# Converting float64 weights on the chip: the sign enters with the integer addition instead of in a pass of its own

## The chip, the cores and the metric

The kernel runs on one core of a Trainium2 chip. What counts is the device time of one execution in microseconds (us). The engines of the core are named as in the profile: PE (TensorE, matmuls; PEld is its weight load), DVE (VectorE), ACT (ScalarE), POOL (GpSimd) and SP (SyncE, which only issues DMAs here).

## The reference, cut to what matters

A causal attention with decay over 4 batches of 8 heads (576 rows, 64 columns each), followed by two feed-forward layers without bias:

```python
attn = softmax(q @ k.T / 8 + decay, causal) @ v      # -> x of 2304 x 512
x = square(relu(x @ w_in)) @ w_out                   # 512 -> 2048 -> 512
h = x @ w2_in
out = where(h >= 1, h, where(h <= -1, 0, (h + 1)**2 / 4)) @ w2_out
```

The four weight matrices reach the kernel as float64, seen as pairs of 32-bit words. The kernel turns each number into a float32 and then into a sum of two numbers that PE takes (a high and a low part), so that three matmuls stand for one precise product.

## The kernel before, in words

The 2304 rows are cut into five blocks of 512, 512, 512, 512 and 256 columns of PE's moving operand. Each block goes through 32 steps: 16 for the first layer pair and 16 for the second. A step is 12 matmuls into `h` (line 1009), an activation on ACT and DVE (lines 1027 to 1040, and the difference `gl` on line 586 or 588), and, two steps later, 12 matmuls into the four accumulators (lines 1060 to 1062). The attention of a block runs between the steps of the block ahead of it. For the first 256 rows of a head it is `attention32` (matmuls on lines 646, 675 and 689), for the others `attention`.

Only block 0 meets weights that are still float64. For each of its steps one piece of up to 1024 columns is loaded (`raw`), decoded (`decode`, into `wf`), and split into its high and low part (`w_split`, into `whl`). `whl` is used from SBUF in that step, and also stored in DRAM (`scr`), from where blocks 1 to 4 load it again. So all decoding lies in the first 262 us. There are 34 pieces: most of 1024 columns, a few of 512.

A piece is decoded in these passes over its columns, where `lo` and `hi` are the two words of a float64:

- `o1` (line 940 on ACT or 941 on DVE): the absolute value of `hi`, into `wf`.
- `o2` (line 944 on ACT or 945 on POOL): the top bits of `lo`, scaled down, into `low`.
- `o3` (line 948, DVE): clamp between F32_MIN and F32_MAX.
- `o4` (line 950, DVE): shift left by 5, then right by 2.
- `o5` (line 952, DVE): sign and top exponent bit, masked out of `hi`, are put in with an "or".
- the addition (line 955 on DVE or 956 on POOL): `wf` plus `low`, as integers.

Then `w_split` copies the high part (line 574 on ACT, 577 on DVE) and subtracts it (line 586 on DVE, 588 on POOL). There is one `low` buffer, two `wf` buffers, and six buffers that `raw` and `whl` share.

No order is written out by hand. Each operation names the engines that it could run on, with an assumed cost for each; `Schedule.improve` plays the whole program through with several sets of weights, chooses engine and order for every operation, and the program is emitted in that order. Any change of an operation or of a cost can therefore move operations all over the kernel.

Of the kernel before, what the change touches and what calls it, by code (L numbers as in the profile page):

```python
# [8 lines left out]
F32 = mybir.dt.float32  # L9
F32R = mybir.dt.float32r  # L10
F16 = mybir.dt.float16
BF16 = mybir.dt.bfloat16
I32 = mybir.dt.int32
U32 = mybir.dt.uint32
U64 = mybir.dt.uint64
AF = mybir.ActivationFunctionType
ALU = mybir.AluOpType
# [4 lines left out]
P = 128  # L22
# [37 lines left out]
def pattern(bits):  # L60
    return struct.unpack("f", struct.pack("I", bits))[0]


F32_MIN = pattern(0x38100000)
F32_MAX = pattern(0x47EFFFFF)


# [278 lines left out]
def act_t(n, psum=False, ptr=0):  # L346
    return n / 1200.0 + (0.05 if psum else 0.095) + 0.095 * ptr


def dve_t(n):  # L350
    return n / 960.0 + 0.07


def dve2_t(n):
    return n / 1920.0 + 0.065


def pool_t(n):
    return n / 1200.0 + 0.18


def pool2_t(n):
    return n / 467.0 + 0.13
# [17 lines left out]
def tile_attention_moe_moe(ctx: ExitStack, tc: tile.TileContext, qkv, f, blank, w2, outT):  # L381
    nc = tc.nc
    PSUM = bass.MemoryType.PSUM
    W64 = w2.dtype == U64
    sch = Schedule()
    const = ctx.enter_context(tc.tile_pool(name="const", bufs=1))
# [8 lines left out]
    def new(tag, name, shape=None, dt=None, kind=None):  # L395
        p, tp, sh, d = pools[tag]
        shape = sh if shape is None else shape
        kw = {"padded_shape": sh} if list(shape) != list(sh) and len(shape) == len(sh) and dt is None else {}
        return Buf(p, lambda: tp.tile(shape, dt or d, tag=tag, name=name, **kw), kind)
# [50 lines left out]
    for blk in range(5):  # L450
        lo, hi = (T_LO, T_START) if blk == 0 else (V[NFC * ATTENTION[blk][0]], V[NFC * ATTENTION[blk][1]] - 6)
# [12 lines left out]
    mask = const.tile([P, OFF + P], BF16, name="mask")  # L464
    half = const.tile([P, 1], F32, name="half")
    warm = const.tile([P, 1], F32, name="warm")
    ident = const.tile([P, P], F32, name="ident")
    Q2 = [const.tile([P, REST], F32R, name=f"Q2_{i}") for i in range(2)]
    K2 = [const.tile([P, S], F32R, name=f"K2_{i}") for i in range(2)]

    QK = [new("PT", f"QK{i}", [P, QUAD * 2 * HEAD], F32) for i in range(2)]

    def setup():
        sb = new("x", "setup", [P, 2 * NKC * 512], F32)
# [2 lines left out]
        lb = lambda a=D, z=P, c=0, m=1: sb.tile[a:z, 4 * S + HEAD * c:4 * S + HEAD * (c + m)]  # L477
        due = -100.0
        G, V_, A = nc.gpsimd, nc.vector, nc.scalar
        oh = sch.op(due - 10, {"POOL": (0.05, lambda: G.memset(warm, 0.5))})  # L480
        oh = sch.op(due - 10, {"ACT": (1.5, lambda: A.activation(warm, warm, AF.Ln))}, [oh])

        bs = []
        for i, (a, z) in enumerate(((0, 1), (1, QUAD))):
            n = (z - a) * HEAD
# [8 lines left out]
        o2 = sch.op(due - 5, {"POOL": (0.55, lambda: G.memset(onesf(0, P), 1.0))}, bufs=[sb])  # L494
        sch.op(due + 90, {"POOL": (0.05, lambda: G.memset(half, 0.5))})
        o3 = sch.op(due, {"DVE": (0.37, lambda: V_.tensor_scalar(
            fr(), fr(), 1e-4, 1.0, op0=ALU.max, op1=ALU.min))}, [o1], [sb])
        o4 = sch.op(due, {"ACT": (0.58, lambda: A.activation(lf(), fr(), AF.Ln))}, [o3, oh], [sb])
        o5 = sch.op(-98.5, {"DVE": (0.67, lambda: V_.tensor_tensor_scan(
            cum(), onesf(), lf(), 0.0, op0=ALU.mult, op1=ALU.add))}, [o4, o2], [sb])  # L500
        sch.op(due, {"ACT": (1.4, lambda: A.activation(warm, warm, AF.Exp))}, [o4, *bs])
        hi = lambda: fr().bitcast(F32R)
        lo = lambda: lf().bitcast(F32R)
        o6 = sch.op(due + 125, {"DVE": (0.37, lambda: V_.tensor_copy(hi(), cum()))}, [o5], [sb])
# [6 lines left out]
        def first_rows(head, row, out, deps):  # L511
            return sch.op((-101, -99, 8, 8)[head], {"DVE": (0.61, lambda: V_.tensor_tensor_scan(
                out(), onesf(row, row + 1, HEAD), lb(row, row + 1, head), 0.0, op0=ALU.mult, op1=ALU.add))},
                [bs[head > 0], o2, *deps], [sb, QK[0]])

        zs = {}
        due = 100.0
# [33 lines left out]
    def clear(i, half):  # L551

        n = QUAD * HEAD
        rows = lambda a, z: QK[i].tile[a:z, n * half:n * half + n]
        kq = lambda a, z, t: rows(a, z).rearrange("p (c t n) -> p c t n", t=2, n=HEAD)[:, :, t, :]
        if i + half:
            return [sch.op(-90, {"SP": (dma_t(D * n * 4), lambda: nc.sync.dma_start(out=rows(D, P), in_=blank))},
                           [], [QK[i]], early=BE[2 * i + half - 1])]
        fill = lambda out, x: {"DVE": (n / 1920 + 0.01, lambda: nc.vector.memset(out(), x))}
# [10 lines left out]
    def copies(out, in_, n, engines="ACT DVE POOL", psum=False):  # L570

        alts = {}
        if "ACT" in engines:
            alts["ACT"] = (act_t(n, psum), lambda: nc.scalar.activation(out(), in_(), AF.Copy))  # L574
        if "DVE" in engines:
            alts["DVE"] = (
                dve_t(n) if psum else dve2_t(n), lambda: nc.vector.tensor_copy(out(), in_()), *([] if psum else [True]))
        if "POOL" in engines:
            alts["POOL"] = (pool_t(n), lambda: nc.gpsimd.tensor_scalar(  # L579
                out(), in_(), 1.0, 0.0, op0=ALU.mult, op1=ALU.add))  # L580
        return alts

    def subs(out, a, b, n, engines="DVE POOL"):
        alts = {}
        if "DVE" in engines:
            alts["DVE"] = (dve_t(n), lambda: nc.vector.tensor_sub(out(), a(), b()), True)  # L586
        if "POOL" in engines:
            alts["POOL"] = (pool2_t(n), lambda: nc.gpsimd.tensor_sub(out(), a(), b()))  # L588
        return alts
# [302 lines left out]
    scr_op, raw, wf, whl, whl_op, new_pairs = {}, {}, {}, {}, {}, {}  # L892

    def span(layers):
        return slice(layers[0], layers[-1] + 1)

    def w_load(s):
# [10 lines left out]
        if first:  # L908
            b = new("big", f"raw{s}", [P, 2, 512], U64) if W64 else new("wf", f"wf{s}")
            loads = []  # L910
# [20 lines left out]
    def decode(words, y, n, due, loads, rb, w):  # L931


        lo, hi = lambda: words()[:, :, 0], lambda: words()[:, :, 1]
        yi = lambda: y().bitcast(I32)
        lb = new("low", f"low{w.order}")
        part = lambda: lb.tile[:, :n]
        v = nc.vector
        o1 = sch.op(due, {
            "ACT": (act_t(n), lambda: nc.scalar.activation(y(), hi().bitcast(F32), AF.Abs)),  # L940
            "DVE": (dve2_t(n), lambda: v.tensor_scalar(yi(), hi(), 0x7FFFFFFF, None, op0=ALU.bitwise_and), True),
        }, loads, [rb, w])
        o2 = sch.op(due, {
            "ACT": (act_t(n), lambda: nc.scalar.activation(part(), lo().bitcast(U32), AF.Copy, scale=2.0 ** -29)),
            "POOL": (pool_t(n), lambda: nc.gpsimd.tensor_scalar(
                part(), lo().bitcast(U32), 2.0 ** -29, 0.0, op0=ALU.mult, op1=ALU.add)),
        }, loads, [rb, lb])
        o3 = sch.op(due + 0.6, {"DVE": (dve2_t(n), lambda: v.tensor_scalar(
            y(), y(), F32_MIN, F32_MAX, op0=ALU.max, op1=ALU.min), True)}, [o1], [w])
        o4 = sch.op(due + 1.2, {"DVE": (dve2_t(n), lambda: v.tensor_scalar(  # L950
            yi(), yi(), 5, 2, op0=ALU.logical_shift_left, op1=ALU.logical_shift_right), True)}, [o3], [w])
        o5 = sch.op(due + 2.4, {"DVE": (dve_t(n), lambda: v.scalar_tensor_tensor(  # L952
            yi(), hi(), -0x40000000, yi(), op0=ALU.bitwise_and, op1=ALU.bitwise_or), True)}, [o4], [rb, w])
        return sch.op(due + 4.8, {
            "DVE": (dve_t(n) + 0.07, lambda: v.tensor_tensor(yi(), yi(), part(), op=ALU.add), True),  # L955
            "POOL": (pool2_t(n), lambda: nc.gpsimd.tensor_tensor(yi(), yi(), part(), op=ALU.add)),
        }, [o5, o2], [lb, w])

    def w_decode(s):
        if s not in raw:  # L960
# [13 lines left out]
    def w_split(s):  # L974

        if s not in wf:
            return
        c = span(sorted(layer for layers in new_pairs[s].values() for layer in layers))
        n = 512 * (c.stop - c.start)
        w = wf.pop(s)  # L980
        if s not in whl:
            whl[s] = new("big", f"whl{s}")
        b = whl[s]
        due = V0(s + 2) - 4.5
        hi, lo = (lambda i=i: b.tile[:, c, i, :] for i in range(2))
        o = sch.op(due, copies(hi, lambda: w.tile[:, c], n, "ACT DVE"), whl_op[s], [w, b])
        o = sch.op(due + 1, subs(lo, lambda: w.tile[:, c], lambda: hi().bitcast(F32), n), [o], [w, b])
        whl_op[s].append(o)
        for pair, layers in new_pairs[s].items():
            c_ = span(layers)  # L990
            store = sch.op(due + 6, {"SP": (dma_t(P * 4096 * len(layers)), lambda c_=c_, pair=pair: nc.sync.dma_start(
                out=scr[pair][:, c_], in_=b.tile[:, c_].bitcast(F32)))}, [o], [b])
            for layer in layers:
                scr_op[pair, layer] = store
# [200 lines left out]
```

## Time and profile before

| | us |
|---|---|
| median of 3 runs | 969.46 (968.41 to 970.44) |
| the profiled execution, its time | 967.33 |
| the profiled execution, its span | 965.6 |
| PE busy | 939.4 (97%) |
| ACT busy | 631.0 (65%) |
| DVE busy | 605.0 (63%) |
| POOL busy | 192.6 (20%) |

The span is the part of the time that the trace covers. Busy shares are averages over stages: DVE is busy nine tenths or more of nearly every slice up to 260 us, and between one and seven tenths after that. A matmul's record is longer than the distance to the next one, since matmuls overlap, so that small gaps of PE don't show as idle time. Records of neighbours on DVE and ACT overlap a little too.

### The profile page before, as it was taken

What the parts mean: (1) busy time and instruction counts of PE and PEld (TensorE: products, weight loads), DVE (VectorE), ACT (ScalarE), POOL (GpSimd) and SP (SyncE); (2) the same over time, 40 slices, a digit from 0 to 9 for tenths busy, and PEclk for the clock granted to TensorE, in tenths of its full rate; (3) what the DMA queues carried; (4) which work ended last, traced back from release to release, by engine and by line L of the source; (5) the groups of instructions that cost most, each with busy time, mean ns of one, the idle gap of its engine ahead of it and who ended that gap; (6) DMA issues with size and microseconds to landing.
All of it is one profiled execution on the core that took longest, in us unless ns stands there. A gap on an engine that the chain in (4) does not pass through costs nothing.

```text
span 965.6 us, 14315 instructions
## 1 busy us (share of the span) xinstructions
PE 939.4 (97%) x4758; PEld 782.6 (81%) x4758; DVE 605.0 (63%) x1338; ACT 631.0 (65%) x1274; POOL 192.6 (20%) x329
## 2 busy tenths in 40 slices
PE   6999999998999999999999999999999999999998
PEld 4767777766778888888888888888888888889998
DVE  7999999999966868767677767776311132220032
ACT  5999888777676777877677777776433343334354
POOL 4210202232223233333222222332000000002200
PEclk7999999999999999999999999999999999999999
DMA  7789998987999898898799888888565555559993
GB/s 190 244 283 411 365 346 299 318 327 270 360 263 325 249 275 229 249 277 255 210 291 265 270 274 208 234 255 220 196 224 209 178 203 190 188 205 354 370 377 142
DMA packets 126618, 255.77 MB, mean 265 GB/s; under 512 B 89880, under 2 KB 90800, under 8 KB 104592
## 3 DMA queue, kind: packets, MB, share of 16 engines
q1 hardware_dynamic: 126544, 254.85, 82.3%
q8 instruction: 38, 0.62, 0.3%
q14 instruction: 36, 0.29, 0.1%
HBM read 195.40 MB, written 38.45 MB: 242 GB/s over the span
## 4 chain that ended last, share of the span: by engine, by line
PE 80%; DVE 9%; DMA 3%; issue 2%; ACT 2%; SPq 0%; POOL 0%; DVEq 0%; ACTq 0%; POOLq 0%
PE h L1009 35%; PE acc L1060 12%; PE acc L1062 12%; PE acc L1061 12%; PE av L846 4%; PE s L767 2%; PE s L768 2%; DVE wf L952 2%; DMA PT<-PP 2%; DVE whl L586 1%; DVE wf L955 1%; DVE gl L586 1%; DVE wf L950 1%; DMA out_dram<-o 1%; ACT whl L574 1%
## 5 line engine op out<-in xcount | busy, mean ns | idle before, releaser
L1009 PE MATMUL h<-x,whl 128*128 128x512 f32 (+1 forms) x1896 | 433.6, 372 | 7.9 <-DVE whl L586 6.4
L1009 PEld LDWEIGHTS h<-x,whl 128*128 128x128 f32 x1896 | 324.7, 189 | 66.2 <-DVE whl L586 9.4
L1060 PE MATMUL acc<-gh,whl 128*128 128x512 f32 (+1 forms) x640 | 239.8, 375 | 2.3 <-ACT o L574 2.3
L1062 PE MATMUL acc<-gl,whl 128*128 128x512 f32 (+1 forms) x640 | 236.9, 370 | 0.3 <-DVE gl L586 0.2
L1061 PE MATMUL acc<-gh,whl 128*128 128x512 f32 (+1 forms) x640 | 236.4, 369 | 0.2 <-DVE whl L586 0.2
L586 DVE TENSOR_TENSOR gl<-g,gh 128x512 fp32r<-128x512 f32 (+1 forms) x119 | 79.6, 669 | 113.3 <-PE acc L1062 81.7
L1062 PEld LDWEIGHTS acc<-gl,whl 128*128 128x128 f32 x640 | 120.7, 189 | 21.9 <-DVE gl L586 0.7
L1060 PEld LDWEIGHTS acc<-gh,whl 128*128 128x128 f32 x640 | 120.8, 189 | 21.5 <-ACT o L574 3.2
L1061 PEld LDWEIGHTS acc<-gh,whl 128*128 128x128 f32 x640 | 120.8, 189 | 16.1 <-DVE whl L586 0.7
L588 POOL TENSOR_TENSOR gl<-g,gh 128x512 fp32r<-128x512 f32 (+1 forms) x41 | 45.9, 1120 | 287.7 <-PE acc L1062 214.5
L1040 DVE SCALAR_TENSOR_TENSOR g<-r,h 128x512 f32<-128x512 f32 (+1 forms) x80 | 50.5, 631 | 80.3 <-ACT r L1038 79.5
L1027 ACT ACTIVATE r<-h 128x512 f32<-128x512 f32 (+1 forms) x80 | 44.0, 550 | 84.1 <-PE h L1009 81.4
L1036 ACT ACTIVATE r<-h,half 128x512 f32<-128x512 f32 (+1 forms) x80 | 51.2, 640 | 65.4 <-PE h L1009 64.2
L821 DVE SCALAR_TENSOR_TENSOR PP<-E,st,PP 128x512 f16<-128x512 f32 (+2 forms) x128 | 75.1, 620 | 12.0 <-ACT PP L817 11.6
L784 ACT ACTIVATE E<-E,st 64x320 f32<-64x320 f32 (+2 forms) x96 | 63.7, 664 | 25.5 <-DVE st L593 16.9
L817 ACT ACTIVATE PP<-E,st 128x512 f16<-128x512 f32 (+2 forms) x128 | 68.9, 591 | 9.0 <-DVE st L791 4.6
L593 DVE CUSTOM_DVE_ANT_0 E<-s,mask 128x288 f32<-128x288 f32 (+2 forms) x128 | 61.9, 500 | 20.0 <-PE s L768 17.4
L846 PEld LDWEIGHTS av<-pr,vt 128*128 128x128 f32 x288 | 53.2, 188 | 13.6 <-ACT r L1036 1.4
L574 ACT ACTIVATE gh<-g 128x512 fp32r<-128x512 f32 (+1 forms) x73 | 42.5, 582 | 32.0 <-DVE g L1040 31.8
L846 PE MATMUL av<-pr,vt 128*128 128x320 f32 (+2 forms) x288 | 61.8, 287 | 0.9 <-DVE st L593 0.7
L574 ACT ACTIVATE pr<-PT 128x640 fp32r<-128x640 f16 (+2 forms) x64 | 37.0, 587 | 30.3 <-DMA PT<-PP 25.7
L579 POOL TENSOR_SCALAR pr<-PT 128x640 fp32r<-128x640 f16 (+2 forms) x45 | 29.4, 657 | 117.6 <-PE av L846 56.4
(251 smaller groups left out, 1148.5 us busy)
## 6 DMA issues: line engine op xcount, KB each, us to landing
whl<-scr SPq DMA_DIRECT2D x112, 1024.0 KB
raw<-in_w_dram SPq DMA_DIRECT2D x28, 1024.0 KB
scr<-whl SPq DMA_DIRECT2D x28, 1024.0 KB
in<-in_qkv_dram SPq DMA_DIRECT2D x32, 608.0 KB
whl<-scr SPq DMA_DIRECT2D x32, 512.0 KB
out_dram<-o SPq DMA_DIRECT2D x16, 256.0 KB
QK<-in_qkv_dram SPq DMA_DIRECT2D x7, 512.0 KB
raw<-in_w_dram SPq DMA_DIRECT2D x6, 512.0 KB
```

Of the source, the lines that this page charges most:

```text
L574: alts["ACT"] = (act_t(n, psum), lambda: nc.scalar.activation(out(), in_(), AF.Copy))
L586: alts["DVE"] = (dve_t(n), lambda: nc.vector.tensor_sub(out(), a(), b()), True)
L593: return nc.vector.tensor_tensor_reduce(out=out, in0=ps, in1=mask[:m, OFF - q0:OFF - q0 + n], scale=scale, scalar=3e38, op0=ALU.add, op1=A ...
L784: nc.scalar.activation(Ec.tile[:m, :e], Ec.tile[:m, :e], AF.Exp, scale=-1.0, bias=nmx(), accum_out=st.tile[:m, 1, ci:ci + 1])))}, [*tops, ...
L817: nc.scalar.activation(hi, x, AF.Copy, scale=r())
L821: nc.vector.scalar_tensor_tensor(lo, x, r(), hi, op0=ALU.mult, op1=ALU.subtract)
L846: nc.tensor.matmul(av.tile[:, c0:W], vt.tile[:, kc, :, :], pr.tile[:, i, :n], start=(kc == 0 and i == 0), stop=(kc == NK - 1))
L1009: nc.tensor.matmul(ps.tile[:, :n], w.tile[:, 0, wi, kc * P:(kc + 1) * P], src.tile[:, kc, xi, :n], start=(kc == 0 and i == 0), stop=(kc == ...
L1036: o1 = sch.op(due, {"ACT": (act_t(n, True, 1), lambda: A.activation(r.tile[:, :n], ps(), AF.Relu, scale=0.5, bias=half))}, [o], [psb, r])
L1060: nc.tensor.matmul(a.tile[:, :n], wh, gh.tile[:, :n], start=(fc == 0), stop=False)
L1061: nc.tensor.matmul(a.tile[:, :n], wl, gh.tile[:, :n], start=False, stop=False)
L1062: nc.tensor.matmul(a.tile[:, :n], wh, gl.tile[:, :n], start=False, stop=(fc == NFC - 1))
```

## The change

`o5` is gone. A new pass `o6` fills the upper 16 bits of each word of `low` with the sign and the constant exponent bits 0x3F80, either on ACT (the function Sign, written as bf16, which is 0x3F80 or 0xBF80; a small `tiny` is added so that zero counts as positive) or on DVE (mask and "or" on the topmost 16-bit quarter of the float64). `o2` writes only the lower 16 bits of `low`, and its second engine is DVE in place of POOL. `o4` shifts left by 3 and no longer right. So the one integer addition puts in sign, exponent and low bits. Because the decoded number is now half of what it was, `w_split` doubles it: its copy gets a scale, and its subtraction becomes a `scalar_tensor_tensor` on DVE, with POOL no longer a choice. `tiny` is filled once by POOL at the start.

```diff
-F32_MIN = pattern(0x38100000)
+F32_MIN = pattern(0x38200000)
...
+        tiny_op.append(sch.op(due - 9, {"POOL": (0.05, lambda: G.memset(tiny, 2.0 ** -30))}))
...
         o2 = sch.op(due, {
-            "ACT": (act_t(n), lambda: nc.scalar.activation(part(), lo().bitcast(U32), AF.Copy, scale=2.0 ** -29)),
-            "POOL": (pool_t(n), lambda: nc.gpsimd.tensor_scalar(
-                part(), lo().bitcast(U32), 2.0 ** -29, 0.0, op0=ALU.mult, op1=ALU.add)),
+            "ACT": (act_t(n), lambda: A.activation(part16(0), lo().bitcast(U32), AF.Copy, scale=2.0 ** -29)),
+            "DVE": (dve2_t(n), lambda: v.tensor_scalar(
+                part16(0), lo().bitcast(U32), 2.0 ** -29, None, op0=ALU.mult), True),
         }, loads, [rb, lb])
+        o6 = sch.op(due, {
+            "ACT": (act_t(n, ptr=1), lambda: A.activation(
+                part16(1).bitcast(BF16), hi().bitcast(F32), AF.Sign, bias=tiny)),
+            "DVE": (dve2_t(n), lambda: v.tensor_scalar(
+                part16(1), words16()[:, :, 3], 0x8000, 0x3F80, op0=ALU.bitwise_and, op1=ALU.bitwise_or), True),
+        }, [*loads, *tiny_op], [rb, lb])
...
         o4 = sch.op(due + 1.2, {"DVE": (dve2_t(n), lambda: v.tensor_scalar(
-            yi(), yi(), 5, 2, op0=ALU.logical_shift_left, op1=ALU.logical_shift_right), True)}, [o3], [w])
-        o5 = sch.op(due + 2.4, {"DVE": (dve_t(n), lambda: v.scalar_tensor_tensor(
-            yi(), hi(), -0x40000000, yi(), op0=ALU.bitwise_and, op1=ALU.bitwise_or), True)}, [o4], [rb, w])
+            yi(), yi(), 3, None, op0=ALU.logical_shift_left), True)}, [o3], [w])
...
-        }, [o5, o2], [lb, w])
+        }, [o4, o2, o6], [lb, w])
...
-        o = sch.op(due, copies(hi, lambda: w.tile[:, c], n, "ACT DVE"), whl_op[s], [w, b])
-        o = sch.op(due + 1, subs(lo, lambda: w.tile[:, c], lambda: hi().bitcast(F32), n), [o], [w, b])
+        src, unit = lambda: w.tile[:, c], 2.0 if W64 else 1.0
+        o = sch.op(due, {
+            "ACT": (act_t(n), lambda: nc.scalar.activation(hi(), src(), AF.Copy, scale=unit)),
+            "DVE": (dve2_t(n), lambda: nc.vector.tensor_scalar(hi(), src(), unit, None, op0=ALU.mult), True),
+        }, whl_op[s], [w, b])
+        o = sch.op(due + 1, {"DVE": (dve_t(n), lambda: nc.vector.scalar_tensor_tensor(
+            lo(), src(), unit, hi().bitcast(F32), op0=ALU.mult, op1=ALU.subtract), True)}, [o], [w, b])
```

## Rows read from the trace of the kernel before

**Rows 1.** The page's first part: engine, busy us (share of the span), instructions.

```profile
PE 939.4 (97%) x4758; PEld 782.6 (81%) x4758; DVE 605.0 (63%) x1338; ACT 631.0 (65%) x1274; POOL 192.6 (20%) x329
```

**Rows 2.** Busy time by stretch; the first line names the columns.

```profile
core 0: us, PE busy (x) PEld busy (x) DVE busy (x) ACT busy (x) POOL busy (x), PEclk, DMA share, GB/s
26.00:260.00 234.00, 224.34 (x1073) 172.75 (x1074) 226.12 (x416) 196.40 (x375) 48.31 (x48) 1.00 0.88 320
...
80.00:100.00 20.00, 20.00 (x95) 15.67 (x95) 18.98 (x28) 18.27 (x28) 1.29 (x1) 1.00 0.98 391
```

**Rows 3.** The chain that ended last: start us, us, what it spent them on.

```profile
45.55 1.15 DVE wf L952
...
49.98 1.14 DVE whl L586
```

**Rows 4.** Waits, 20 to 260 us: us in total, times, longest us.

```profile
POOL low L945 <- DVE wf L955: 81.3, 9, 17.8
...
PE h L1009 <- DVE whl L586: 6.4, 7, 1.6
```

**Rows 5.** The chain again, where no weights are decoded: two neighbouring steps.

```profile
711.62 2.72 PE h L1009 x12
...
717.07 2.72 PE h L1009 x12
```

**Rows 6.** PE's timeline: first matmul of step 0 and of step 32.

```profile
38.25 0.94 PE L1009 MATMUL h<-x,whl-2_523 128*128 128x512 f32 x3
...
253.69 1.07 PE L1009 MATMUL h<-x,whl 128*128 128x512 f32 x4
```

**Rows 7.** PE and PEld busy in these stretches, lines 1009, 646, 675, 689 in turn.

```profile
38.00:253.60 215.60, 100.27 (x384) 69.49 (x385) 1.00 0.89 325
...
44.00:253.60 209.60, 11.27 (x54) 8.96 (x54) 1.00 0.88 323
...
44.00:253.60 209.60, 8.89 (x51) 6.59 (x51) 1.00 0.88 323
...
44.00:253.60 209.60, 9.16 (x72) 3.83 (x72) 1.00 0.88 323
```

**Rows 8.** Busy by stretch of lines 952 (DVE), 945 (POOL), 944, 940 (ACT).

```profile
26.00:260.00 234.00, 40.35 (x33) 1.00 0.88 320
...
26.00:260.00 234.00, 15.94 (x13) 1.00 0.88 320
...
26.00:260.00 234.00, 21.15 (x19) 1.00 0.88 320
...
26.00:260.00 234.00, 35.75 (x32) 1.00 0.88 320
```

**Rows 9.** Timeline of DVE and ACT: start us, duration us, instruction.

```profile
93.06 1.06 ACT L574 ACTIVATE whl<-wf 128x1024 fp32r<-128x1024 f32 x1 [1.12 <-issue]
93.61 0.70 DVE L950 TENSOR_SCALAR wf<-wf 128x1024 int32<-128x1024 int32 x1
94.03 1.14 ACT L944 ACTIVATE low<-raw 128x1024 int32<-128x1024 uint32 x1
94.22 1.22 DVE L586 TENSOR_TENSOR whl<-wf,whl 128x1024 fp32r<-128x1024 f32 x1
...
95.36 1.22 DVE L952 SCALAR_TENSOR_TENSOR wf<-raw,wf 128x1024 int32<-128x1024 int32 x1
```

**Rows 10.** Groups by line: count, busy us, mean ns, idle before.

```profile
L941 DVE TENSOR_SCALAR wf-1_322<-raw-1_258 128x512 int32<-128x512 int32 x1 | 0.4, 418 | 0.0
L588 POOL TENSOR_TENSOR whl-2_523<-wf-2_249,whl-2_523 128x512 fp32r<-128x512 f32 x1 | 1.3, 1312 | 0.6 <-DVE whl-2_523 L577 0.6
L1036 ACT ACTIVATE r<-h,half 128x512 f32<-128x512 f32 x16 | 10.9, 682 | 5.3 <-PE h L1009 5.2
L1027 ACT ACTIVATE r<-h 128x512 f32<-128x512 f32 x17 | 10.0, 588 | 0.9 <-PE h L1009 0.7
L501 ACT ACT_TABLE_LOAD x1 | 1.3, 1283 | 0.0
```

More of the change, by code (lines that the diff above doesn't have):

```diff
@@ L14 @@
 U32 = mybir.dt.uint32
+U16 = mybir.dt.uint16
 U64 = mybir.dt.uint64
@@ L466, in tile_attention_moe_moe @@
     warm = const.tile([P, 1], F32, name="warm")
+    tiny = const.tile([P, 1], F32, name="tiny")
     ident = const.tile([P, P], F32, name="ident")
@@ L471, in tile_attention_moe_moe @@
     QK = [new("PT", f"QK{i}", [P, QUAD * 2 * HEAD], F32) for i in range(2)]
+    tiny_op = []
     def setup():
@@ L937, in decode @@
         part = lambda: lb.tile[:, :n]
-        v = nc.vector
+        part16 = lambda i: part().bitcast(U16).rearrange("p (n t) -> p n t", t=2)[:, :, i]
+        top = lambda: hi().bitcast(U32)
+        v, A = nc.vector, nc.scalar
         o1 = sch.op(due, {
-            "ACT": (act_t(n), lambda: nc.scalar.activation(y(), hi().bitcast(F32), AF.Abs)),
+            "ACT": (act_t(n), lambda: A.activation(y(), hi().bitcast(F32), AF.Abs)),
             "DVE": (dve2_t(n), lambda: v.tensor_scalar(yi(), hi(), 0x7FFFFFFF, None, op0=ALU.bitwise_and), True),
@@ L943, in decode @@
         o2 = sch.op(due, {
-            "ACT": (act_t(n), lambda: nc.scalar.activation(part(), lo().bitcast(U32), AF.Copy, scale=2.0 ** -29)),
-            "POOL": (pool_t(n), lambda: nc.gpsimd.tensor_scalar(
-                part(), lo().bitcast(U32), 2.0 ** -29, 0.0, op0=ALU.mult, op1=ALU.add)),
+            "ACT": (act_t(n), lambda: A.activation(part16(0), lo().bitcast(U32), AF.Copy, scale=2.0 ** -29)),
+            "DVE": (dve2_t(n), lambda: v.tensor_scalar(
+                part16(0), lo().bitcast(U32), 2.0 ** -29, None, op0=ALU.mult), True),
         }, loads, [rb, lb])
+        o6 = sch.op(due, {
[4 more added lines that the diff above has]
+        }, [*loads, *tiny_op], [rb, lb])
+        words16 = lambda: words().rearrange("p n t -> p (n t)").bitcast(U16).rearrange("p (n t) -> p n t", t=4)
         o3 = sch.op(due + 0.6, {"DVE": (dve2_t(n), lambda: v.tensor_scalar(
```

## The prediction, made before the changed kernel had run

> **What bounds the kernel now.** I read the page's busy line first, then the stage in which weights are decoded, then the chain and the waits of that stage, then PE's pace with and without decoding. The busy line says that PE is the limit: 97% of the span, DVE 63% [rows 1]. That average hides two stages. From 26 to 260 us DVE is busy 226.12 of 234 us (97%) and ACT 196.40 (84%), while PE has 9.7 us without a record [rows 2]. After that DVE is mostly free, and the edit touches nothing there. So the change is worth what it brings before 260 us. The chain agrees: near the start it runs from one decoding pass on DVE to the next, line 952 among them [rows 3]; the only wait of PE for decoded weights that the list of waits shows is small, 6.4 us [rows 4].
>
> How much can PE gain there? Undisturbed, a step starts 5.45 us after the one ahead of it (717.07 - 711.62) [rows 5]. Steps 0 to 31 are 384 matmuls into `h`, all recorded, and take from 38.25 to 253.69, that is 215.4 us [rows 6, 7]. 32 x 5.45 are 174.4; the attention matmuls among them add 11.27 + 8.89 + 9.16 = 29.3 [rows 7]. That is 203.7, so PE loses 11.7 us. Since attention's records overlap a little, and the last passes reach past step 32, I put the most that can come back at 15.
>
> **The change part by part, from 26 to 260 us.** A pass costs the distance to the next start, a little less than its record: DVE's quick pass (line 950) of 1024 columns is 0.70 us long and the next starts 0.61 later, its plain one 1.22 and 1.14; on ACT the next starts 0.97 after a pass of 1.06 [rows 9]. So I take 0.09 off each record.
>
> `o5` goes: 33 passes, 40.35 us of records less 33 x 0.09, which is 37.4 off DVE [rows 8]. `o4` keeps its form, and so does the addition; I cost the fewer bits that they handle at nothing. The subtraction in `w_split` turns from tensor_tensor (1.22) into scalar_tensor_tensor (1.22, as line 952) [rows 9]: nothing. POOL did it for one half-wide piece (1.31) [rows 10]; on DVE that is about half of 1.14, so 0.6. DVE without the new passes: 226.1 - 37.4 + 0.6 = 189.3.
>
> New to ACT and DVE are 46 passes: 33 of `o6`, and the 13 of `o2` that POOL did [rows 8]. On ACT, `o2` costs 21.15/19 - 0.09 = 1.02 and `o6` 35.75/32 - 0.09 = 1.03 and the price of the bias read from `tiny`. The rows show no Sign; a pass of 512 columns with such a bias takes 682 ns and one without 588 [rows 10], so I add 0.09. The mean over 46 is 1.09. On DVE no row shows 16-bit halves read or written with gaps between them. The nearest is line 941, which reads every second 32-bit word: 418 ns for 512 columns [rows 10], the pace of 0.70 for 1024. Its distances in bytes are those of `o6`, so I take 0.61; the other end is the plain pace, 1.13. Neither end allows a gain: the passes weren't there.
>
> If a of the 46 go to DVE, DVE has 189.3 + 0.61 a and ACT 196.4 + 1.09 (46 - a). Both are 210 at a = 34. Against today's 226.1 that takes 16 us off the busiest engine. At 1.13 they meet at a = 26 and 218.5, and 7.6 come off. It turns at 27 passes on ACT, 19 on DVE: there ACT has 226, what DVE has now. All 46 on ACT would be 246.5.
>
> [...]
>
> What takes a wait: `low` is a single buffer, and `o2` waits for the last addition to let go of it. Today that wait is mostly POOL's, 81.3 us in all, and costs nothing, since little stands behind it [rows 4]. On ACT, what queues behind a waiting `o2` or `o6` is Relu and Square of `h`, for which PE's second half-step waits; on DVE, `gl`, with the same waiter. The planner places it late enough in its own times; a wait on the chip costs at most the rest of one addition, 1.2 us. `raw` is free again earlier, after `o1`, `o2` and `o6` rather than behind three DVE passes, so SP can issue the next load earlier. DMA carries that: 320 GB/s over the stage, 391 in its fullest stretch [rows 2], and 15 us less make 320 x 234/219 = 342. The memset of `tiny` stands ahead of little on POOL, about 0.1 us, in a time when PE waits for attention's loads.
>
> Before 26 us two half-wide pieces are decoded: their `o5` goes and two short `o6` come. I cost that at nothing, bounded by 0.7 us a piece either way.
>
> **The sum.** DVE loses 16 us of load, PE can take back 11.7 to 15. Two engines at 210 of a stage of some 225 us are both over 90% busy, and each piece passes from one to the other five times, so some waits stay. I take two thirds of 11.7: 8 us. The profiled execution would go from 967.33 to 959.3; the median of the runs lies 2.1 above the profiled one, so 969.46 becomes 961.5.
>
> **The rivals.**
>
> ACT becomes the bound (slower). In the rows the planner put 32 of `o1`'s passes on ACT in this stage, where DVE was a choice too [rows 8]; for it speaks that habit, against it that DVE's place is then emptier and its pass cheaper. From 27 of 46 passes on ACT there is no gain; at 36 ACT has 235.6, 9.5 us over today's bound, and PE waits for `r` and `gh`: 979. All 46 give 20 us: 990.
>
> Nothing comes of it. PE has few gaps in view, 6.4 us of wait for `whl` [rows 4], and the planner lays the whole kernel out anew: what DVE gives up could be lost where attention's passes now fall. Price: 2 us either way, 967.5 to 971.5.
>
> All comes back: PE runs at its own pace through the stage, 12 to 16 us, so 953.5 to 957.5.
>
> The half-word passes run at the plain pace or slower: 7.6 off the bound in place of 16, half of the forecast's gain, 965.5.
>
> Sign needs another table than Exp. Abs, Relu, Square, Copy and Exp follow the load on line 501 with no other, and a load takes 1.28 us [rows 10]. If Sign isn't in that table, each Sign between other functions costs two loads, 2.57 us. With 15 of them on ACT, 38 us come to an engine near its limit: some 30 us more, 1000.
>
> [...]
>
> **How the numbers follow.** Forecast, 4 to 12 us gained: 0.50. All comes back: 0.13. Plain pace: 0.10. Nothing: 0.15. ACT the bound: 0.09. Tables: 0.03. A measurement of this kernel can tell about 0.2% (1.9 us) from no change. Faster: 0.50 + 0.13 + 0.09 + a fifth of 0.15, 0.75. Same: two thirds of 0.15 and a little of the plain pace and of ACT's case, 0.12. Slower: the rest, 0.13. The range runs from the lower end of the full gain, 953.5, to the upper end of no change, 971; it leaves out the tables, most of ACT's case and a part of the full gain below it, some 0.16.
>
> **What would show it.** Line 952 gone; DVE under 93% from 26 to 250 us and ACT over 87%; the 46 passes split with at least 19 on DVE, at 0.70 us for 1024 columns there, and Sign near 1.2 us on ACT; step 32 starting near 246 rather than 253.69; the stages behind it as long as before; no third table load. Wrong would be: DVE as busy as before with PE's gaps where they were (then DVE's load wasn't the cause), ACT at 97% with PE waiting for `r` or `gh`, or a loss after 260 us, which would be the planner's new order and no effect of the passes.

## The result, and the profile after

| | before | after |
|---|---|---|
| median, us | 969.28 (968.41 to 970.44, 4 runs) | 958.83 (956.66 to 960.36, 4 runs) |
| the profiled execution, its time | 967.33 | 959.39 |
| its span | 965.6 | 957.6 |

The ratio is 0.989, with a 95% interval of 0.9867 to 0.9912: 10.5 us less. The forecast was 961.5, in a range from 953.5 to 971.0.

The busy line of the changed kernel's page, to be read against [rows 1], and the first line of part 4 of both pages, the chain that ended last by engine: before first, then after.

```profile
PE 938.3 (98%) x4758; PEld 785.4 (82%) x4758; DVE 594.7 (62%) x1341; ACT 641.9 (67%) x1273; POOL 179.5 (19%) x328
```

```profile
PE 80%; DVE 9%; DMA 3%; issue 2%; ACT 2%; SPq 0%; POOL 0%; DVEq 0%; ACTq 0%; POOLq 0%
```

```profile
PE 92%; DMA 3%; ACT 2%; DVE 2%; issue 0%; SPq 0%; DVEq 0%; ACTq 0%
```

The chain has left DVE: 9% of the span before, 2% after, and PE has 92% of it.

Now the stretches, busy us of PE, PEld, DVE, ACT and POOL (columns as in [rows 2]): before the change, then after it. The stretch from 26 to 250 us is the one in which both kernels decode throughout.

```profile
0.00:26.00 26.00, 16.99 (x83) 12.32 (x83) 18.67 (x62) 14.83 (x43) 11.86 (x29) 0.80 0.78 207
26.00:250.00 224.00, 214.34 (x1026) 164.70 (x1026) 216.61 (x399) 187.78 (x357) 43.04 (x42) 1.00 0.88 318
250.00:300.00 50.00, 47.97 (x227) 39.12 (x226) 36.10 (x86) 35.66 (x76) 11.87 (x22) 1.00 1.07 310
300.00:580.00 280.00, 278.95 (x1344) 234.18 (x1343) 203.64 (x512) 206.91 (x434) 86.62 (x169) 1.00 0.91 261
```

```profile
0.00:26.00 26.00, 16.02 (x66) 11.76 (x67) 17.31 (x50) 14.85 (x37) 10.39 (x27) 0.74 0.79 198
26.00:250.00 224.00, 219.18 (x1061) 169.80 (x1060) 211.05 (x424) 201.47 (x365) 37.63 (x44) 0.99 0.89 327
250.00:300.00 50.00, 50.00 (x242) 42.19 (x241) 36.50 (x91) 36.43 (x80) 11.63 (x25) 1.00 0.95 272
300.00:580.00 280.00, 280.00 (x1351) 236.25 (x1350) 201.90 (x504) 209.47 (x436) 81.66 (x168) 1.00 0.89 263
```

From them comes the ledger of PE's idle time. Before 26 us it grew from 9.0 to 10.0; from 26 to 250 it fell from 9.7 to 4.8; from 250 to 300 from 2.0 to none; to 580 from 1.05 to none. That is 6.9 of the 8.0 us by which the span shrank. The other 1.1 us is PE's busy time itself, 939.4 before and 938.3 after; whether those are gaps too small to show between overlapping records is not shown. DVE went from 97% to 94% of the stage and ACT from 84% to 90%, while more matmuls fit into it (1061 against 1026).

The new passes, from the groups by form (count, busy us, mean ns) for ACT and from the answer on the tile `low` (shortest, median and longest ns) for DVE. Line 957 is `o6` on ACT, 952 `o2` on ACT, 953 `o2` on DVE, 959 `o6` on DVE.

```profile
L957 ACT ACTIVATE low<-raw,tiny 128x1024 bf16<-128x1024 f32 x18 | 26.4, 1465 | 0.2 <-DVE wf L968 0.2
L952 ACT ACTIVATE low<-raw 128x1024 uint16<-128x1024 uint32 x16 | 21.9, 1370 | 0.1
```

```profile
L953 DVE TENSOR_SCALAR low<-raw x14: 740/768/1270, 45.1 to 232.1; 128x1024 uint16<-128x1024 uint32 x14
L959 DVE TENSOR_SCALAR low<-raw x13: 457/769/785, 63.0 to 238.8; 128x1024 uint16<-128x1024 uint16 x12, 128x512 uint16<-128x512 uint16 x1
```

A pass of 1024 columns that writes 16-bit halves of words is 1370 ns on ACT, 1465 with the bias from `tiny`, and about 769 on DVE. On the same engines whole words took 1.14 and 0.70 us [rows 9].

### The profile page after: what moved, and what is told of

Its sections match the earlier page's. It is cut to its first block, busy times and chain, and to the rows that moved or that the text cites. A ratio compares the mean times of both kernels' runs of the same rounds, so it can differ in the third digit from the quotient of the medians.

```text
span 957.6 us, 14261 instructions
## 1 busy us (share of the span) xinstructions
PE 938.3 (98%) x4758; PEld 785.4 (82%) x4758; DVE 594.7 (62%) x1341; ACT 641.9 (67%) x1273; POOL 179.5 (19%) x328
## 3 DMA queue, kind: packets, MB, share of 16 engines
q1 hardware_dynamic: 126544, 254.85, 81.3%
## 4 chain that ended last, share of the span: by engine, by line
PE 92%; DMA 3%; ACT 2%; DVE 2%; issue 0%; SPq 0%; DVEq 0%; ACTq 0%
PE h L1027 40%; PE acc L1078 14%; PE acc L1080 13%; PE acc L1079 13%; PE av L851 4%; PE s L772 2%; PE s L773 2%; DMA cumd<-setup 1%; DMA PT<-PP 1%; DMA QK<-in_qkv_dram 1%; PE s1q L651 0%; ACT low L957 0%; PE s7q L651 0%; PE s2q L651 0%; DMA setup<-in_f_dram 0%
## 5 line engine op out<-in xcount | busy, mean ns | idle before, releaser
L591 DVE TENSOR_TENSOR gl<-g,gh 128x512 fp32r<-128x512 f32 (+1 forms) x126 | 84.7, 673 | 121.8 <-PE acc L1080 81.4
L1079 PEld LDWEIGHTS acc<-gh,whl 128*128 128x128 f32 x640 | 120.8, 189 | 15.6
L593 POOL TENSOR_TENSOR gl<-g,gh 128x512 fp32r<-128x512 f32 (+1 forms) x34 | 37.7, 1109 | 322.8 <-PE acc L1080 263.8
L826 DVE SCALAR_TENSOR_TENSOR PP<-E,st,PP 128x512 f16<-128x512 f32 (+2 forms) x128 | 77.2, 640 | 7.8 <-ACT PP L822 7.4
L579 ACT ACTIVATE gh<-g 128x512 fp32r<-128x512 f32 (+1 forms) x68 | 39.4, 579 | 29.1 <-DVE g L1058 28.7
L579 ACT ACTIVATE pr<-PT 128x640 fp32r<-128x640 f16 (+2 forms) x59 | 34.9, 602 | 22.4 <-DMA PT<-PP 20.8
L1056 ACT ACTIVATE r<-r 128x512 f32<-128x512 f32 (+1 forms) x80 | 46.9, 586 | 2.0
```

The source lines that it names most:

```text
L826: nc.vector.scalar_tensor_tensor(lo, x, r(), hi, op0=ALU.mult, op1=ALU.subtract)
L1079: nc.tensor.matmul(a.tile[:, :n], wl, gh.tile[:, :n], start=False, stop=False)
```

## The experiments

**Theory 1**: DVE's load in the decoding stage held PE back, and the change takes load off the busiest engine. **Theory 2**: what counts is that `o2` leaves POOL, whose passes would stretch DVE's: in the kernel before, a pass of line 948 at 111.07 us took 1.43 us beside one of `o2` on POOL, against a median of 0.69. **Theory 3**: the gain is the luck of a new plan, since the planner lays out the whole kernel anew at any change.

### Take the pass away and put nothing in its place

```diff
-        o5 = sch.op(due + 2.4, {"DVE": (dve_t(n), lambda: v.scalar_tensor_tensor(
-            yi(), hi(), -0x40000000, yi(), op0=ALU.bitwise_and, op1=ALU.bitwise_or), True)}, [o4], [rb, w])
...
-        }, [o5, o2], [lb, w])
+        }, [o4, o2], [lb, w])
```

> The kernel before with the pass o5 left out and nothing in its place (weights lose their sign and top exponent bit; the other work is unchanged). Theory 1, DVE's load was what held PE back: DVE's busy time in 26 to 250 us falls by some 37 us, PE takes back nearly all that it can, 954 to 959, a little under the changed kernel's 958.8. Theory 2, the gain comes from POOL's pass o2 leaving POOL (fewer stretched passes on DVE): POOL keeps its 13 passes here, so the time stays at 965 or more. Theory 3, the gain is the luck of a new plan: anywhere from 960 to 972.

Here the weights lose their sign and top exponent bit, and nothing takes the pass's place. Measured: 951.82 us, ratio 0.982 (0.9797 to 0.9843). PE has 220.57 busy of the 224 us from 26 to 250, with POOL's passes still there. That is 2 us more gain than theory 1 had allowed for, and theory 2 falls. It is also the price of `o5` alone, 17 us, as far as one plan can tell it.

### Put a pass back

The changed kernel with one more DVE pass per piece, of `o5`'s form, that changes no value:

```diff
+        o4 = sch.op(due + 2.4, {"DVE": (dve_t(n), lambda: v.scalar_tensor_tensor(
+            yi(), hi(), 0, yi(), op0=ALU.bitwise_and, op1=ALU.bitwise_or), True)}, [o4], [rb, w])
```

> The changed kernel with one more pass on DVE for each piece, of the form and at the place of the old o5 but with a mask of zero, so that it changes no value. Theory 1: 33 x 1.13 = 37 us go back on DVE, which then has some 248 us of work for a stage of 224; slower than before the change, 972 to 985. Theory 2, POOL's share was the cause: 959 to 964, since POOL stays relieved. Theory 3: no bound, but nothing that follows DVE's load.

Measured: 983.55 us, ratio 1.0145 (1.0107 to 1.0184): some 37 us more on DVE cost 25 us against the changed kernel. The list of waits from 20 to 260 us (us in total, times, longest) shows PE waiting for decoded weights again, as in [rows 4]:

```profile
PE h L1029 <- DVE whl L1006: 7.5, 11, 1.8
...
PE h L1029 <- ACT whl L1003: 3.7, 4, 1.5
```

In the changed kernel no wait of PE for `whl` is left; its longest is another (below).

### Take `o2` off POOL, and nothing else

```diff
-            "POOL": (pool_t(n), lambda: nc.gpsimd.tensor_scalar(
-                part(), lo().bitcast(U32), 2.0 ** -29, 0.0, op0=ALU.mult, op1=ALU.add)),
+            "DVE": (dve2_t(n), lambda: v.tensor_scalar(
+                part(), lo().bitcast(U32), 2.0 ** -29, None, op0=ALU.mult), True),
```

> The kernel before, all passes kept, with one part of the change alone: o2's second engine is DVE in place of POOL (whole words, as before). Theory 1 (DVE's load): ACT and DVE take over 13 passes and lose none, so 969 to 977, no faster than before. Theory 2 (POOL's passes stretch DVE's): 962 to 966, since POOL is relieved of 16 us.

Measured: 974.39 us, ratio 1.007 (1.005 to 1.009). This part of the change brings nothing by itself, and theory 2 is out a second time. Whether it costs the 0.7% is less sure: a new plan of unchanged passes alone came to 0.5% (below).

### All the new passes on one engine

The changed kernel with the lines for DVE taken out of `o2` and `o6`, or those for ACT:

```diff
-            "DVE": (dve2_t(n), lambda: v.tensor_scalar(
-                part16(0), lo().bitcast(U32), 2.0 ** -29, None, op0=ALU.mult), True),
...
-            "DVE": (dve2_t(n), lambda: v.tensor_scalar(
-                part16(1), words16()[:, :, 3], 0x8000, 0x3F80, op0=ALU.bitwise_and, op1=ALU.bitwise_or), True),
```

> The changed kernel with o2 and o6 on ACT alone: all 66 passes there rather than 37. Measured so far at 1.37 and 1.46 us each, the 29 moved ones are 38 us more on ACT, 239 us for a stage of 224 to 234, while DVE is relieved of 20. If an engine's load in the stage is what counts, ACT is now the bound and the time is 965 to 980, with PE waiting for r and gh. If only DVE's load counts, 948 to 957.

> The changed kernel with o2 and o6 on DVE alone: 37 passes of some 0.68 us move from ACT to DVE, 25 us, some of it given back by Abs and copies that go to the emptier ACT. Theory 1: DVE has 225 to 234 us of work again, 960 to 970. If the plan's luck decides, no bound.

Measured: on ACT 965.7 us, ratio 0.9985 (0.997 to 0.9999); on DVE 965.15 us, ratio 0.9978 (0.9965 to 0.9991). Nearly the whole gain is gone either way, so the split over two engines is what brings it. The stretch from 26 to 250 us, ACT alone first, then DVE alone:

```profile
26.00:250.00 224.00, 215.58 (x1032) 165.77 (x1031) 194.36 (x399) 217.72 (x363) 41.91 (x46) 0.99 0.87 315
```

```profile
26.00:250.00 224.00, 214.44 (x1025) 165.68 (x1025) 213.40 (x403) 171.39 (x340) 33.93 (x41) 0.99 0.87 317
```

With all on ACT, ACT is busy 217.72 of 224 (97%), where DVE stood before, and DVE has fallen to 87%. PE's gaps are back at 8.4 and 9.6 us. The expectation that PE would then wait for `r` and `gh` held only in part: the list of waits has one of 1.0 us for `r` and none for `gh`; most of the others are for attention's passes, 1.4 us at most.

The busy share alone does not tell these cases apart. With all new passes on DVE it was busy 213.40 of 224 us, and PE had gaps of 9.6 us. In another plan of the split passes (the weights 0.2, 0.35, 0.5 below) it was busy 213.91, and PE had gaps of 1.2:

```profile
26.00:250.00 224.00, 222.80 (x1079) 172.60 (x1079) 213.91 (x425) 201.38 (x362) 35.90 (x45) 1.00 0.91 329
```

What differs is the work for each matmul that PE got done. By these rows DVE had 211 ns of work per matmul before the change (216.61 / 1026), 208 with all passes on DVE, 199 in the changed kernel and 198 in this plan; ACT had 211 with all passes on ACT. PE itself took 206 per matmul where it had hardly a gap (222.80 / 1079). This is rough, since matmuls differ in size, but it sorts these runs: where DVE or ACT needs as long as PE or longer, the gain is gone. The other plans of the old passes are at 206 to 211 on DVE.

### Other plans of the same passes

Only the weights are changed that the planner tries, (0.4, 0.6, 0.8) in both kernels:

```diff
-WEIGHTS = [{}, *({"DVE": x, "POOL": x * y} for x in (0.4, 0.6, 0.8) for y in (0.0, 0.5, 1.0))]
+WEIGHTS = [{}, *({"DVE": x, "POOL": x * y} for x in (0.3, 0.5, 0.7) for y in (0.0, 0.5, 1.0))]
```

The same was done with (0.2, 0.35, 0.5) and (0.45, 0.9, 1.4).

> The kernel before with no operation changed; only the set of weights that the planner tries is another (0.3, 0.5, 0.7 for 0.4, 0.6, 0.8), so that it may settle on another order. Theories 1 and 2: within 2.5 us of 969.3. Theory 3, the order itself is worth many microseconds: it moves by 4 us or more either way.

> The changed kernel with the same other set of weights for the planner. Theories 1 and 2: 957 to 962. Theory 3: 963 or more, most of the gain gone.

> The kernel before with no operation changed and a third set of weights for the planner (0.2, 0.35, 0.5). If a plan is worth 7 us either way whatever the passes, 962 to 976; if the order only matters once DVE's load no longer sets the stage, 966 to 972.

> The changed kernel with the same weights (0.2, 0.35, 0.5). The change is worth some 13 us on the mean of the two plans seen (959 and 952): 950 to 960. If the 952 was an outlier, 957 to 962; if the change's plan of 959 was one that lost to stalls, below 956.

> The kernel before with no operation changed and a fourth set of weights (0.45, 0.9, 1.4), under which the planner gives POOL more. If a plan is worth 7 us either way, 962 to 976; if DVE's load sets the stage, 966 to 972.

> The changed kernel with the weights (0.45, 0.9, 1.4): 950 to 960, and in any case 8 us or more under the kernel before with the same weights. If the gain were the plan's luck, the two would lie within 4 us of each other.

Measured, as ratios to the kernel before on the same chip:

| weights | passes of before | passes of after |
|---|---|---|
| 0.4, 0.6, 0.8 | 1 | 0.989 (0.9867 to 0.9912) |
| 0.3, 0.5, 0.7 | 1.0013 (0.9995 to 1.0031) | 0.9819 (0.9797 to 0.9842) |
| 0.2, 0.35, 0.5 | 1.005 (1.0033 to 1.0067) | 0.9854 (0.982 to 0.9889) |
| 0.45, 0.9, 1.4 | 1.0016 (0.9995 to 1.0038) | 0.9871 (0.9836 to 0.9905) |
| mean | 1.0020 | 0.9859 |

All plans of the changed passes are faster than all plans of the old ones, so theory 3 falls as the cause. The means lie 1.6% apart, some 15.6 us. But a plan is worth some microseconds: up to 0.5% among the old passes, 0.7% among the new, and the plan that the change came with has the highest ratio of its four. Each experiment above has a single plan of its own, too. The second plan of the new passes, 952.01 us in its own comparison, beats both kernels; with it the new passes cost nothing that the end shows, since leaving `o5` out altogether gave 951.82. Its stretch from 26 to 250 us:

```profile
26.00:250.00 224.00, 223.28 (x1084) 174.69 (x1085) 210.29 (x429) 209.23 (x375) 35.70 (x51) 1.00 0.90 335
```

PE is idle for 0.7 us of 224, and DVE (210) and ACT (209) are level, as the sum of the prediction had them.

### Whole words first

`o2` writes 32-bit words again, and `o6` afterwards the upper halves over them:

```diff
-            "ACT": (act_t(n), lambda: A.activation(part16(0), lo().bitcast(U32), AF.Copy, scale=2.0 ** -29)),
+            "ACT": (act_t(n), lambda: A.activation(part(), lo().bitcast(U32), AF.Copy, scale=2.0 ** -29)),
...
-                part16(0), lo().bitcast(U32), 2.0 ** -29, None, op0=ALU.mult), True),
+                part(), lo().bitcast(U32), 2.0 ** -29, None, op0=ALU.mult), True),
...
-        }, [*loads, *tiny_op], [rb, lb])
+        }, [*loads, *tiny_op, o2], [rb, lb])
```

> The changed kernel with o2 writing whole 32-bit words of low, as before, and o6 afterwards writing the upper halves over them (a new order between the two). If the gaps between 16-bit results are what makes ACT's passes 1.37 in place of 1.13, o2 costs 1.13 on ACT and 0.69 on DVE here, and o6 stays at 1.46 and 0.77. Some 18 x 0.24 = 4 us less on ACT: 954 to 959, unless the new order between o2 and o6 costs that.

Measured: 956.02 us, ratio 0.9884 (0.9863 to 0.9905). Groups by form:

```profile
L957 ACT ACTIVATE low<-raw,tiny 128x1024 bf16<-128x1024 f32 x23 | 33.8, 1469 | 0.2
L952 ACT ACTIVATE low<-raw 128x1024 int32<-128x1024 uint32 x21 | 24.0, 1141 | 0.7 <-DVE wf L968 0.7
...
L953 DVE TENSOR_SCALAR low<-raw 128x1024 int32<-128x1024 uint32 x9 | 6.2, 688 | 0.1
L959 DVE TENSOR_SCALAR low<-raw 128x1024 uint16<-128x1024 uint16 x7 | 5.3, 761 | 0.4 <-ACT low L952 0.2
```

`o2` is back at 1141 and 688 ns, `o6` stays at 1469 and 761: the price is that of the 16-bit result with a gap behind it, 0.23 us on ACT and 0.08 on DVE. Whether this version is faster than the change as it came can't be told: its ratio lies within the spread of plans, and it has a plan of its own.

## Why the prediction was right, point by point

**What bounds the kernel.** Right, and shown: without `o5` 17 us go, with a pass put back 25 come. The worth of PE's gaps was put at 11.7 us, 15 at most. That cap was some 2 us low: the best plan took 16.8 by the medians of its own comparison (968.82 to 952.01; 15.4 between the profiled executions), and leaving `o5` out took 17. The cap counted one stage alone, and not all that came back lay there: in the changed kernel 2.0 us from 250 to 300 and 1.05 behind that came back too. The other plan of the old passes (0.3, 0.5, 0.7) is not idle from 250 to 300 either, so those 2.0 belong to the order and not to the passes:

```profile
250.00:300.00 50.00, 50.00 (x237) 41.69 (x236) 37.46 (x91) 35.00 (x72) 13.09 (x25) 1.00 1.04 316
```

The wait of 6.4 us was not the only one of PE for decoded weights either; the list has 1.2 us more for ACT's copies (line 574).

**The prices.** DVE's half-word passes kept the quick pace, 0.77 us against 0.70 forecast; the plain pace, 1.22, is out. ACT's price was the mis-sized term: 1.37 and 1.465 us for records of 1.11 and 1.21. `o6`, with its bias, took 95 ns more than `o2` (1465 - 1370), which is what was forecast for the bias; most of the 0.25 on top is the 16-bit result with gaps, 0.23 us in 1024 columns by the run with whole words, which no row of before showed, and it fell on the `o2` passes that ACT had already, too.

**The split.** Of the 66 passes of `o2` and `o6` from 26 to 250 us 29 ran on DVE (34 were forecast, at least 19 needed; the forecast counted 46, the other 20 being `o2` passes, 19 of which ACT had before), and seven wide copies of the high part moved there too (line 1002). So DVE ended at 94%, not under 93%, and ACT at 90%. The turning point was put at 27 of 46 on ACT and all 46 at 20 us more than before. That was too dear: with all of them on ACT the kernel is as fast as before (0.9985), though each cost more than forecast. The step that failed is that the rest would stay: with ACT that full, the planner put ten copies and six absolute values of 1024 columns on DVE.

**Two thirds of PE's gaps.** The 8 us stood as 7.9 between the profiled executions and as 10.5 between the medians, but the reason given, waits between two engines at over 90%, is not the one found: in the best plan DVE is at 94% and ACT at 93%, and PE is idle for 0.7 us. In the changed kernel PE's longest wait in the stage is a single one of 2.67 us. PE's timeline (idle before in brackets), then DVE and POOL ahead of it, then PE's busy time and granted clock by 2 us:

```profile
216.38 0.69 PE L651 MATMUL s7q<-QK 128*128 128x128 f32 x2 [2.67 <-DVE st7q L598]
```

```profile
211.98 1.58 DVE L591 TENSOR_TENSOR gl<-g,gh 128x512 fp32r<-128x512 f32 x1
...
213.11 1.73 POOL L593 TENSOR_TENSOR K<-in,K 64x576 fp32r<-64x576 f32 x1
213.75 1.64 DVE L1002 TENSOR_SCALAR whl<-wf 128x1024 fp32r<-128x1024 f32 x1 [0.19 <-PE acc L1080]
215.91 0.41 DVE L598 CUSTOM_DVE_ANT_0 E7q<-s7q,mask 128x256 f32<-128x256 f32 x1
```

```profile
214.00:216.00 2.00, 0.00 (x0) 1.00 1.02 430
216.00:218.00 2.00, 1.62 (x5) 0.63 1.01 426
218.00:220.00 2.00, 2.00 (x7) 0.52 0.89 372
```

Two DVE passes whose medians are 0.69 us (lines 591 and 1002) took 1.58 and 1.64 while POOL prepared `K` and `Q`, and PE stood still until the attention pass behind them (line 598) was done. The stretch explains only a part of the wait. By the profile, line 1002 waited for PE's own last matmul before the gap (line 1080), so the first stretched pass delayed nothing; the second took 0.95 us longer than usual. The remaining 1.7 us come from the order of the plan, which put lines 1002 and 1058 ahead of line 598. PE then ran for some 3.5 us at a granted clock near 0.50 (0.50 to 0.56 in each half us from 216.5 to 220), which is about 1.7 us lost by an estimate from the two granted clocks (2 x 0.37 + 2 x 0.48).

Three things make up 7.0 of the 7.5 us between this plan's span and the best one's: these 1.7 us of slow clock, 1.2 us more of idle time before 26 us (16.02 against 17.24 busy), and 4.1 us more of gaps from 26 to 250 (4.8 against 0.7, the 2.67 among them). So the size came out near by luck: the plan lost in a few places of its own about what the estimate had set aside for waits between ACT and DVE. Whether the stretched passes would be quick again with POOL kept out was not tried.

**The rivals.** "Nothing comes of it" and "ACT the bound" are out for this plan; the second is a bound all the same, at 0.9985, if the passes aren't split. "All comes back", 953.5 to 957.5, is what the other three plans of the same passes do: their ratios, times the 969.46 that the forecast started from, give 951.9, 955.3 and 957.0. So it deserved more than its 0.13. "Half-word passes at the plain pace" is out by their 0.77 us. Sign needs no table of its own: the page after shows two loads, each once, as before.

```profile
L486 ACT ACT_TABLE_LOAD x1 | 1.3, 1283 | 0.7 <-PEq L1195 0.7
L506 ACT ACT_TABLE_LOAD x1 | 1.3, 1283 | 0.0
```

**Smaller points.** Step 32 starts 3.3 us sooner, not 7.7, at 250.42 against 253.69 [rows 6]:

```profile
250.42 0.84 PE L1027 MATMUL h<-x,whl 128*128 128x512 f32 x3
```

That mark was a poor one: the plans place attention's matmuls differently around it, and PE's idle time in a stretch says more. The wait for the single `low` buffer, once POOL's 81.3 us [rows 4], cost ACT and DVE next to nothing: 0.4 us in all, in the list of waits.

## What to carry to other kernels

Look for the stage in which an engine is full, not for its share of the whole span: DVE was busy 63% of the kernel, and one of its passes was worth 17 us because of a stage at 97%. Measure that stage by the engine's work for each unit of the bottleneck's work, since a share in a fixed stretch hides how much got done. Work taken off a full engine paid here as far as the next engine filled up, so leave the replacement a choice of two engines; on either one alone the same passes gave nearly nothing (0.9985 and 0.9978). Where a planner lays out the program, run two or three plans of both versions before a difference under 1% is put down to the edit: the four plans of the new passes spread over 0.7%.

## What was not expected of the hardware

- ACT takes 1370 ns for 1024 columns whose 16-bit results have a gap of two bytes between them, and 1141 for the same pass with whole words. That neighbouring 16-bit results cost no more is an estimate from these groups by form of the changed kernel, ACT:

```profile
L822 ACT ACTIVATE PP<-E,st 128x512 f16<-128x512 f32 x64 | 43.1, 708 | 0.0
L1049 ACT ACTIVATE g<-r 128x512 f32<-128x512 f32 x62 | 39.1, 630 | 1.5
```

The fp16 pass has a scale read from SBUF. If that costs the 95 ns that `o6` with its bias took over `o2`, it would take 613 without it, no longer than the 630 of the one with whole words; no run here has the fp16 pass without it. On DVE the same gaps cost 0.08 us (769 against 688 ns).
- After an idle time of 2.67 us in the middle of the kernel PE's granted clock was 0.63 and 0.52 over the next 4 us. In the kernel before the longest gaps of that stage, 1.50 and 1.60 us, show no fall: the clock is 1.00 there. The length of a single gap does not settle it: with all new passes on DVE no wait of PE in the list from 20 to 260 us is longer than 1.8 us, and the clock from 26 to 250 us was 0.99, as in the changed kernel; without `o5` the same list has one of 2.9 us, and the clock of that stretch was 1.00.
